# One change in two places: each transposed tile of the joint attention slots is evicted in one step, and the operands of the last pass are prepared in half-size sums on VectorE with the plain ones on ScalarE and Pool

## The chip, the cores and the metric

The kernel runs on one core of one Trainium2 chip. The metric is the time of one execution in microseconds (us), as the device reports it; the median of the runs counts. TensorE is written PE (its weight loads PEld), VectorE DVE, ScalarE ACT, GpSimd POOL, SyncE SP.

## The reference

Causal attention over 4 batches and 8 heads of 576 tokens and 64 dimensions, with a linear memory beside it, and then a mixture of four experts over the 2304 tokens that come out. Cut to what matters:

```python
scores = scale * q @ k.T            # causal, per batch and head
a = softmax(scores)
q_p = phi(q)                        # elu(q) + 1
mem_out = (q_p @ M_prev) / (q_p @ z_prev + 1e-6)
x = g * mem_out + (1 - g) * (a @ v) # g = sigmoid(beta), per head
...
p = domain_probs / domain_probs.sum(-1)
for e in range(4):                  # x is 2304 x 512, w1 512 x 1024, w2 1024 x 512
    out += p[:, e:e+1] * (relu(x @ w1[e]) @ w2[e])
```

Inputs and outputs are float32. TensorE works on fp32r operands, so an operand is split into a high part and a low part (the value less its high part), and a product is summed from high x high, high x low and low x high.

## The kernel before, in words

The program is written out by hand, one stream of calls, and each engine runs its own instructions in the order in which they are written. Two things are woven together.

**The expert work.** Tokens lie in tiles of 128. Ten tiles form five groups of two, which are worked in 24 phases (a phase is one half of one expert's 1024 columns), and the eight tiles left, 1024 tokens, are worked in a last pass of 8 phases, here called the last pass (`tail_phase`). A phase of a group is `mm1` (tiles `h`, line 851; ACT writes the high part `hh`, line 860, DVE the low part `hl`, line 861), then `mm2` (tiles `y`, line 881; DVE adds to `acc`, line 899). `h` and `y` take turns in three PSUM buffers. Weights arrive by DMA in four buffers `stg`; ACT or POOL writes their high parts `w1h`, `w2h`, and POOL their low parts `w1l`, `w2l` (line 249).

**The attention work** is a list of steps with a slot number and a priority (the table `PR`, the calls of `ev`); sorted by these, they are dealt out between the parts of the phases in proportion to their estimated costs. A *joint* task is one pair of heads over the first two tiles of a batch: 4 slots, and 12 such tasks run one after the other. Each transposes keys (`tk`), queries (`tq`) and mapped queries (`tp`) into a PSUM tile. All of these and the output tile `o` share the tag `to`, which has two buffers, so each takes the buffer of the one before the last. `split_q` and `split_k` evict such a tile: ACT writes the high parts at once, and return a function `lo` with which DVE later writes the low parts (lines 371, 374, 387). A later step runs it. The scores `sp` are reduced on DVE (line 486), ACT takes the exponential (line 500), DVE normalises (line 522), PE transposes into `pt` (line 359), ACT writes `pth` (line 542) and DVE `ptl` (line 543). `j_o` (lines 553 and 557) multiplies by the values; ACT copies half of `o` to `otmp` (line 571), and `add` on DVE (line 584) adds the halves into the tokens.

**The operands of the last pass.** The first product of the last pass is taken with 7 block products instead of 8 on the four quarter blocks of the 1024 tokens. `x_ops` prepares their operands during the last two grouped phases, where only one group is left: three plain ones (`A11`, `A12`, `A22`) and four sums or differences (`S1` to `S4`), each 128x1024 and each with a high part (`put`, a copy) and a low part (a subtraction). In the same stretch `wt_prep` sums and splits the last pass's weights (`tsum`, `wth`, `wtl`). Each product of the last pass goes into a tile `tc`, which ACT copies to `trow` (line 1060).

The call that places the pieces of `x_ops` is this:

```python
for z, (cost, part) in enumerate(ph):
    if z % 3 == 2 and pieces:
        pieces.pop(0)()
```

Of the kernel before, what the change touches and what calls it, by code (L numbers as in the profile page):

```python
# [36 lines left out]
    "o": 7,  # L37
    "jn": [1, -0.45],
    "jp": [2, 7],
    "jlo": 9,  # L40
    "jo": [4, 3],
    "wpe": 1500,
    "wvec": 400,
# [14 lines left out]
def tile_attention_moe(  # L58
# [75 lines left out]
    def f(ap):  # L134
        return ap.bitcast(F32)
# [263 lines left out]
    def t_trq(t):  # L399
        pt = to_tile(f"tq{t.i}")  # L400
        qk, last = t.qk, t.nk == NCH
        w = len(t.cs) * P
        for i in range(len(t.cs)):

            tr(pt[:, i * P : (i + 1) * P], flat(t.nat["q"][:, i]), P)
        if last:
            tr(pt[:, w : w + P], flat(t.nat["k"][:, 4]), P)
        t.lo_q = [split_q(pt, qk["qa"], qk["qb"], w, SCALE)]
        if last:
            t.lo_q.append(split_k(pt[:, w:], qk, 4 * P, D))  # L410
            t.lo_q.append(lambda: dup_k(qk, 4 * P, D))
        t.lo_q.append(lambda: dup_q(qk, w, last))

    def dup_q(qk, w, last):
        for h, (x, q_) in enumerate(((A, qk["qa"]), (Bh, qk["qb"]))):
            nc.sync.dma_start(
                out=f(qk["qz"][x, h * GW : (h + 1) * GW]), in_=f(q_[x, 0:GW])
            )
            if last:
                o = 2 * GW + h * D  # L420
                nc.sync.dma_start(out=f(qk["qz"][x, o : o + D]), in_=f(q_[x, w - D : w]))
# [319 lines left out]
    def run(fns):  # L741
        for fn in fns:
            fn()

    seen = set()
    for t in tasks:
        s0 = t.s0
        ld = s0 - 9 if t.i < 1 else s0 - 7
        PQ = PR
        if t.run not in seen:  # L750
            seen.add(t.run)
            ev(s0 - 9, 9, lambda r=t.run: batch_load(r))
# [12 lines left out]
        ev(s0 + PQ["trk"][0], 0.5, lambda t=t: run(t.lo_k))
        ev(
            s0 + PQ["trk"][0] + 1,
            -0.7,
            lambda t=t: dup_k(t.qk, 0, min(t.nk, NCH - 1) * P),
        )  # L770
# [210 lines left out]
    def x_ops():  # L981

        X, s_ = tail["x"], tail["s"]
        s3 = tail["r"][:, 0:2]


        def put(n, src, eng):
            hi, lo = X[n]
            eng.tensor_copy(hi, src)
            eng.tensor_tensor(lo, src, f(hi), ALU.subtract)  # L990

        def plain(n, i, k):
            return [lambda: put(n, a_blk(i, k), nc.vector)]

        def summed(n, eng, dst, a, b, op):
# [5 lines left out]
        return (
            plain("A11", 0, 0)
            + summed("S1", nc.vector, s_, a_blk(1, 0), a_blk(1, 1), ALU.add)
            + summed("S2", nc.vector, s_, s_, a_blk(0, 0), ALU.subtract)
            + summed("S4", nc.vector, s_, a_blk(0, 1), s_, ALU.subtract)
            + summed("S3", nc.vector, s3, a_blk(0, 0), a_blk(1, 0), ALU.subtract)
            + plain("A12", 0, 1)
            + plain("A22", 1, 1)
        )
# [367 lines left out]
    with tc.manual_schedule():  # L1377
# [43 lines left out]
        for n, ph in enumerate(phases):  # L1421
# [53 lines left out]
```

## Time and profile before

| what | value |
|---|---|
| median of 3 runs | 1061.68 us (1061.44 to 1062.12) |
| profiled execution, its own time | 1062.06 us |
| its span in the trace | 1060.3 us |
| PE busy | 998.6 us, 94% |
| DVE busy | 691.1 us, 65% |
| ACT, POOL busy | 542.2 and 545.7 us, 51% each |
| mean granted clock of TensorE | 0.977 of full speed |

Busy time is the time in which an engine has an instruction under way; a matmul's end is modelled, and matmuls overlap. The granted clock is the share of TensorE's full speed that it was given. The span is the time between the first and the last record; 1.8 us of the execution's own time lie outside it.

### The profile page before, as it was taken

The page shows a single profiled execution, that of the slowest core. Times are in us where ns is not written, and L with a number is a line of the kernel's source. Part 1 is how long each engine was busy: PE and PEld are TensorE (multiplying, and loading weights), DVE is VectorE, ACT ScalarE, POOL GpSimd, SP SyncE. Part 2 cuts the span into 40 slices and gives each one's busy share as a digit, 9 for nine tenths or more (in the row PEclk, how much of TensorE's full clock was granted, in tenths as well). Part 3 has the DMA queues.
Part 4 walks back from the last instruction along what each step waited for, and adds up shares of the span by engine and source line. Part 5 has one row for each costly group of instructions (what it writes and reads, how often), then busy time and mean ns, then how long its engine had stood idle before and what let it go on. Part 6 is the DMA issues. An engine that isn't in the chain of part 4 may idle for free.

```text
span 1060.3 us, 15727 instructions
## 1 busy us (share of the span) xinstructions
PE 998.6 (94%) x5072; PEld 830.6 (78%) x5072; DVE 691.1 (65%) x1613; ACT 542.2 (51%) x1240; POOL 545.7 (51%) x593
## 2 busy tenths in 40 slices
PE   5887888998999999999999999978999999999998
PEld 3666767877888887888888888866888888888886
DVE  5776788887776777778777766498444444543532
ACT  4666655665766666667666666434242241331320
POOL 4757665566446574555665455576335245235220
PEclk8989889999999999999999999989999999999999
DMA  5546534455453445444544432344112112112102
GB/s 135 135 125 160 145 108 128 116 137 139 116 134 107 110 115 136 115 108 106 160 117 114 107 101 68 100 130 129 50 50 70 40 41 80 40 40 73 29 19 79
DMA packets 192513, 106.33 MB, mean 100 GB/s; under 512 B 99632, under 2 KB 170800, under 8 KB 192432
## 3 DMA queue, kind: packets, MB, share of 16 engines
q1 hardware_dynamic: 191760, 105.07, 36.4%
q8 instruction: 40, 0.66, 0.3%
q14 instruction: 41, 0.34, 0.1%
q10 hardware_dynamic: 672, 0.27, 0.1%
HBM read 90.09 MB, written 4.72 MB: 89 GB/s over the span
## 4 chain that ended last, share of the span: by engine, by line
PE 74%; DVE 14%; POOL 3%; ACT 3%; issue 2%; DMA 2%; SPq 1%; ACTq 0%; POOLq 0%; DVEq 0%
PE y L881 17%; PE yt L1100 16%; PE h L851 13%; PE tc_1X L1049 4%; PE tc_0X L1049 4%; PE pt L359 3%; PE o L724 3%; PE sp L613 3%; PE tc_1Y L1049 2%; PE tc_0Y L1049 2%; DVE s L522 2%; DVE hl L861 1%; DMA stg<-in_moe_w_dram 1%; POOL w2l L249 1%; PE tc_0Z L1049 1%
## 5 line engine op out<-in xcount | busy, mean ns | idle before, releaser
L249 POOL TENSOR_TENSOR w1l<-stg,w1h 128x512 fp32r<-128x512 f32 x96 | 127.8, 1338 | 199.6 <-ACT w1h L246 194.7
L249 POOL TENSOR_TENSOR w2l<-stg,w2h 128x512 fp32r<-128x512 f32 x128 | 170.5, 1334 | 30.8 <-ACT w2h L246 22.1
L851 PE MATMUL h<-xh,w1h 128*128 128x512 f32 (+1 forms) x384 | 149.5, 389 | 0.4 <-DVE acc L899 0.4
L881 PE MATMUL y<-w2h,hh 128*128 128x512 f32 x320 | 139.2, 435 | 1.5 <-DVE hl L861 1.5
L851 PE MATMUL h<-xh,w1l 128*128 128x512 f32 (+1 forms) x384 | 138.4, 361 | 0.0
L851 PE MATMUL h<-xl,w1h 128*128 128x512 f32 (+1 forms) x384 | 138.1, 360 | 0.0
L881 PE MATMUL y<-w2h,hl 128*128 128x512 f32 x320 | 129.3, 404 | 7.2 <-DVE hl L861 7.2
L881 PE MATMUL y<-w2l,hh 128*128 128x512 f32 x320 | 128.6, 402 | 2.9 <-POOL w2l L249 2.9
L1113 DVE SCALAR_TENSOR_TENSOR xt<-yt,pn,xt 128x512 f32<-128x512 f32 x56 | 42.0, 751 | 87.0 <-PE yt L1100 87.0
L861 DVE SCALAR_TENSOR_TENSOR hl<-h,hh 128x512 fp32r<-128x512 f32 (+1 forms) x96 | 57.6, 600 | 62.8 <-ACT hh L860 61.9
L248 POOL TENSOR_SCALAR w2h<-stg 128x512 fp32r<-128x512 f32 x104 | 65.2, 627 | 58.2 <-PE yt L1100 45.2
L656 ACT ACTIVATE s<-s,st 128x384 f32<-128x384 f32 (+2 forms) x80 | 55.1, 688 | 72.0 <-DVE st L651 71.7
L851 PEld LDWEIGHTS h<-xh,w1l 128*128 128x128 f32 x384 | 73.6, 192 | 11.0
L851 PEld LDWEIGHTS h<-xh,w1h 128*128 128x128 f32 x384 | 74.5, 194 | 7.2 <-ACT qb L368 0.6
L881 PEld LDWEIGHTS y<-w2h,hl 128*128 128x128 f32 x320 | 61.6, 192 | 22.3 <-DVE hl L861 8.6
L851 PEld LDWEIGHTS h<-xl,w1h 128*128 128x128 f32 x384 | 74.4, 194 | 5.4
L860 ACT ACTIVATE hh<-h 128x512 fp32r<-128x512 f32 (+1 forms) x96 | 50.3, 524 | 53.4 <-PE h L851 52.5
L899 DVE SCALAR_TENSOR_TENSOR acc<-y,pn,acc 128x512 f32<-128x512 f32 x70 | 52.3, 747 | 37.6 <-PE y L881 37.2
L881 PEld LDWEIGHTS y<-w2l,hh 128*128 128x128 f32 x320 | 62.3, 195 | 11.9 <-POOL w2l L249 4.7
L359 PE MATMUL pt<-ident,s 128*128 128x128 f32 (+1 forms) x376 | 62.5, 277 | 8.0 <-DVE s L522 4.6
L881 PEld LDWEIGHTS y<-w2h,hh 128*128 128x128 f32 x320 | 62.0, 194 | 10.1 <-DVE hl L861 2.1
L359 PEld LDWEIGHTS pt<-ident,s 128*128 128x128 f32 (+1 forms) x376 | 46.4, 141 | 27.4 <-issue 9.0
(297 smaller groups left out, 2591.5 us busy)
## 6 DMA issues: line engine op xcount, KB each, us to landing
stg<-in_moe_w_dram SPq DMA_DIRECT2D x256, 256.0 KB, 2.9
natall<-in_k_dram SPq DMA_DIRECT2D x34, 128.0 KB, 2.6
natall<-in_v_dram SPq DMA_DIRECT2D x32, 128.0 KB, 3.0
natall<-in_q_dram SPq DMA_DIRECT2D x60, 64.0 KB, 2.6
out_dram<-acc SPq DMA_DIRECT2D x10, 256.0 KB, 2.1
kha<-kha SPq DMA_DIRECT2D x16, 128.0 KB, 2.4
khb<-khb SPq DMA_DIRECT2D x16, 128.0 KB, 2.3
natall<-in_k_dram SPq DMA_DIRECT2D x28, 64.0 KB, 2.5
```

The costliest lines, as they stand in the source:

```text
L248: nc.gpsimd.tensor_scalar(hi, t, 1.0, 1.0, ALU.mult, ALU.mult)
L249: nc.gpsimd.tensor_tensor(lo, t, f(hi), ALU.subtract)
L359: nc.tensor.transpose(dst, src, ident[0:n, 0:n])
L656: nc.scalar.activation(s.s[:, 0:w], s.s[:, 0:w], AF.Copy, scale=s.st[:, 3:4])
L851: nc.tensor.matmul(pt[0][:, cols], lhsT=w_[:, c], rhs=x_[:, c, cols], start=(c == 0 and z == 0), stop=(c == NKD - 1 and z == 2),)
L860: nc.scalar.activation(h_, pt[0][:, cols], AF.Relu)
L861: nc.vector.scalar_tensor_tensor(l_, pt[0][:, cols], 0.0, f(h_), ALU.max, ALU.subtract)
L881: nc.tensor.matmul(pt[0], lhsT=h_[fc][:, tk], rhs=w_, start=(fc == 0 and z == 0), stop=(fc == HF - 1 and z == 2),)
L899: nc.vector.scalar_tensor_tensor(acc[g, tt], pt[0], pe, acc[g, tt], ALU.mult, ALU.add)
L1049: nc.tensor.matmul(bank[b][:, 0:TB], lhsT=w_[:, n, cs], rhs=x_[:, c], start=first and c == 0 and z == 0, stop=c == 1 and z == 2, skip_grou ...
L1100: nc.tensor.matmul(o, lhsT=h_[fc][:, tk], rhs=w_, start=(z == 0 and fc == p and y == 0), stop=(z == 1 and fc == p + 2 and y == 2),)
L1113: nc.vector.scalar_tensor_tensor(acc_, o, pe, acc_, ALU.mult, ALU.add)
```

## The change

In the joint slots the eviction of a tile is no longer divided between two places of the list: the step with the low parts gets the priority of the transposes (`lo_q`, `lo_k`, `lo_qp`, and `lo` of `pt`), and `add` follows `j_o` in its slot instead of the next one. The mapped queries are transposed a slot later (`jtrqp`). The DMAs of `dup_q` become a step of their own. The other attention tasks keep their places. In `x_ops` each sum is made in two halves of 128x512 on DVE, three instructions each; the high parts of the plain operands are copied by ACT, their low parts subtracted by POOL; the pieces are now 30 instead of 11, and two are placed in every three parts of a phase.

```diff
+    "jtrqp": [2, 2.5],
...
-    "jlo": 9,
...
         if last:
             t.lo_q.append(split_k(pt[:, w:], qk, 4 * P, D))
-            t.lo_q.append(lambda: dup_k(qk, 4 * P, D))
-        t.lo_q.append(lambda: dup_q(qk, w, last))
 
     def dup_q(qk, w, last):
+        if last:
+            dup_k(qk, 4 * P, D)
...
-        ev(s0 + PQ["trq"][0], PQ["trq"][1], lambda t=t: t_trq(t), 109.0 * len(t.cs))
-        ev(s0 + PQ["trq"][0] + 1, 0.4, lambda t=t: run(t.lo_q))
-        ev(s0 + PQ["trk"][0], PQ["trk"][1], lambda t=t: t_trk(t), 109.0 * t.nk)
-        ev(s0 + PQ["trk"][0], 0.5, lambda t=t: run(t.lo_k))
...
+        (q0, q1), (k0, k1), j_ = PQ["trq"], PQ["trk"], t.joint
+        ev(s0 + q0, q1, lambda t=t: t_trq(t), 109.0 * len(t.cs))
+        ev(*((s0 + q0, q1) if j_ else (s0 + q0 + 1, 0.4)), lambda t=t: run(t.lo_q))
+        ev(s0 + q0 + 1, 0.45, lambda t=t: dup_q(t.qk, len(t.cs) * P, t.nk == NCH))
+        ev(s0 + k0, k1, lambda t=t: t_trk(t), 109.0 * t.nk)
+        ev(s0 + k0, k1 if j_ else 0.5, lambda t=t: run(t.lo_k))
...
-        ev(s0 + PQ["trqp"][0], PQ["trqp"][1], lambda t=t: t_trqp(t), 109.0 * len(t.cs))
-        ev(s0 + PQ["trqp"][0], 4.5, lambda t=t: run(t.lo_qp))
+        p0, p1 = PQ["jtrqp" if j_ else "trqp"]
+        ev(s0 + p0, p1, lambda t=t: t_trqp(t), 109.0 * len(t.cs))
+        ev(s0 + p0, p1 if j_ else 4.5, lambda t=t: run(t.lo_qp))
...
-            ev(i + PQ["jp"][0], PQ["jlo"], lambda i=i: run(slots[i].lo))
+            ev(i + PQ["jp"][0], PQ["jp"][1], lambda i=i: run(slots[i].lo))
...
-                ev(i + PQ["jo"][0] + 1, -0.6, lambda i=i: run(slots[i].add))
+                ev(i + PQ["jo"][0], PQ["jo"][1], lambda i=i: run(slots[i].add))
...
+        vec = nc.vector.tensor_tensor
+        plain = {"A11": a_blk(0, 0), "A12": a_blk(0, 1), "A22": a_blk(1, 1)}
+
+        def hi(n):
+            return [lambda: nc.scalar.activation(X[n][0], plain[n], AF.Copy)]
+
+        def lo(n):
             return [
+                lambda: nc.gpsimd.tensor_tensor(X[n][1], plain[n], f(X[n][0]), ALU.subtract)
             ]
...
+        def summed(n, dst, a, b, op):
+            h_, l_ = X[n]
+            return [
+                fn
+                for k in range(2)
+                for fn in (
+                    lambda k=k: vec(dst[:, k], a[:, k], b[:, k], op),
+                    lambda k=k: nc.vector.tensor_copy(h_[:, k], dst[:, k]),
+                    lambda k=k: vec(l_[:, k], dst[:, k], f(h_[:, k]), ALU.subtract),
+                )
+            ]
...
+        other = hi("A11") + hi("A12") + lo("A11") + hi("A22") + lo("A12") + lo("A22")
+        out_ = []
+        for z, fn in enumerate(sums):
+            out_.append(fn)
+            if z % 4 == 3:
+                out_ += [other.pop(0)]
+        return out_ + other
...
-                if z % 3 == 2 and pieces:
+                if z % 3 and pieces:
                     pieces.pop(0)()
```

**The order on DVE in a joint task.** A stretch of DVE's row in the joint part of the program before the change, from the low parts of one tile to the next normalisation (`tq` holds queries, `tp` mapped queries, `xr` the tokens):

```order
L371 SCALAR_TENSOR_TENSOR qpa_86<-tp_1042,qpa_86 64x256
L374 SCALAR_TENSOR_TENSOR qpb_87<-tp_1042,qpb_87 64x256
L486 ISA s_1078,st_1079<-sp_1080,mask 128x256
L486 ISA st_1079 128x1
L486 ISA s_1078,st_1079<-sp_1080,mask 128x256
L486 ISA st_1079 128x1
L861 SCALAR_TENSOR_TENSOR hl_113<-h_2_1066,hh_109 128x256
L371 SCALAR_TENSOR_TENSOR qa_91<-tq_1061,qa_91 64x256
L374 SCALAR_TENSOR_TENSOR qb_92<-tq_1061,qb_92 64x256
L861 SCALAR_TENSOR_TENSOR hl_114<-h_3_1096,hh_110 128x256
L543 TENSOR_TENSOR ptl_100<-pt_1139,pth_99 128x2x128
L584 TENSOR_TENSOR xr<-o_1104,otmp_1115 64x256 x2
```

And the same twelve places on DVE in the changed program:

```order
L371 SCALAR_TENSOR_TENSOR qa_91<-tq_1042,qa_91 64x256
L374 SCALAR_TENSOR_TENSOR qb_92<-tq_1042,qb_92 64x256
L486 ISA s_1067,st_1068<-sp_1069,mask 128x256
L486 ISA st_1068 128x1
L486 ISA s_1067,st_1068<-sp_1069,mask 128x256
L486 ISA st_1068 128x1
L861 SCALAR_TENSOR_TENSOR hl_113<-h_2_1061,hh_109 128x256
L371 SCALAR_TENSOR_TENSOR qpa_86<-tp_1093,qpa_86 64x256
L374 SCALAR_TENSOR_TENSOR qpb_87<-tp_1093,qpb_87 64x256
L861 SCALAR_TENSOR_TENSOR hl_114<-h_3_1098,hh_110 128x256
L584 TENSOR_TENSOR xr<-o_1107,otmp_1118 64x256 x2
L543 TENSOR_TENSOR ptl_100<-pt_1141,pth_99 128x2x128
```

The low parts of `tq` and `tp` have changed places, and `add` (line 584) stands ahead of `ptl` (line 543) instead of behind it.

**The order on POOL at the end of the grouped phases.** Before the change, from the first weights of the last grouped phase on:

```order
L249 TENSOR_TENSOR w1l_116<-stg_8037,w1h_115 128x512
L249 TENSOR_TENSOR w1l_118<-stg_8059,w1h_117 128x512
L249 TENSOR_TENSOR w1l_120<-stg_8080,w1h_119 128x512
L249 TENSOR_TENSOR w1l_122<-stg_8099,w1h_121 128x512
L249 TENSOR_TENSOR w2l_124<-stg_8103,w2h_123 128x512
L249 TENSOR_TENSOR w2l_126<-stg_8124,w2h_125 128x512
L249 TENSOR_TENSOR w2l_128<-stg_8128,w2h_127 128x512
L249 TENSOR_TENSOR w2l_130<-stg_8149,w2h_129 128x512
```

In the changed program the same stretch of POOL's row reads:

```order
L249 TENSOR_TENSOR w1l_116<-stg_8039,w1h_115 128x512
L249 TENSOR_TENSOR w1l_118<-stg_8061,w1h_117 128x512
L993 TENSOR_TENSOR A11l<-xt,A11h 128x1024
L249 TENSOR_TENSOR w1l_120<-stg_8082,w1h_119 128x512
L249 TENSOR_TENSOR w1l_122<-stg_8103,w1h_121 128x512
L249 TENSOR_TENSOR w2l_124<-stg_8107,w2h_123 128x512
L249 TENSOR_TENSOR w2l_126<-stg_8128,w2h_125 128x512
L249 TENSOR_TENSOR w2l_128<-stg_8132,w2h_127 128x512
L993 TENSOR_TENSOR A12l<-xt,A12h 128x1024
L249 TENSOR_TENSOR w2l_130<-stg_8153,w2h_129 128x512
L993 TENSOR_TENSOR A22l<-xt,A22h 128x1024
```

Three subtractions of 128x1024 now stand among the weights' low parts, two of them ahead of weights that TensorE still needs in that phase.

**The order on DVE in the same stretch.** Before the change, from the first piece of `x_ops` on:

```order
L989 CAST A11h<-xt 128x1024
L990 TENSOR_TENSOR A11l<-xt,A11h 128x1024
L861 SCALAR_TENSOR_TENSOR hl_111<-h_0_8000,hh_107 128x256
L997 TENSOR_TENSOR xsum<-xt 128x1024
L861 SCALAR_TENSOR_TENSOR hl_112<-h_1_8021,hh_108 128x256
L989 CAST S1h<-xsum 128x1024
L990 TENSOR_TENSOR S1l<-xsum,S1h 128x1024
L997 TENSOR_TENSOR xsum<-xsum,xt 128x1024
L861 SCALAR_TENSOR_TENSOR hl_113<-h_2_8043,hh_109 128x256
```

In the changed program the same stretch of DVE's row reads:

```order
L1003 TENSOR_TENSOR xsum<-xt 128x512
L1004 CAST S1h<-xsum 128x512
L861 SCALAR_TENSOR_TENSOR hl_111<-h_0_8000,hh_107 128x256
L1005 TENSOR_TENSOR S1l<-xsum,S1h 128x512
L1003 TENSOR_TENSOR xsum<-xt 128x512
L861 SCALAR_TENSOR_TENSOR hl_112<-h_1_8022,hh_108 128x256
L1004 CAST S1h<-xsum 128x512
L1005 TENSOR_TENSOR S1l<-xsum,S1h 128x512
L1003 TENSOR_TENSOR xsum<-xsum,xt 128x512
L861 SCALAR_TENSOR_TENSOR hl_113<-h_2_8044,hh_109 128x256
```

Ahead of the third `hl` stood six instructions of 128x1024; now seven of 128x512 stand there.

## Rows read from the trace of the kernel before

**Rows 1.** The page, busy time (us, share of the span, instructions) of each engine.

```profile
PE 998.6 (94%) x5072; PEld 830.6 (78%) x5072; DVE 691.1 (65%) x1613; ACT 542.2 (51%) x1240; POOL 545.7 (51%) x593
```

**Rows 2.** Windows of 100 us: length, busy by engine, granted clock, DMA.

```profile
100.00:200.00 100.00, 86.91 (x483) 73.42 (x481) 81.03 (x212) 60.20 (x163) 65.29 (x77) 0.93 0.47 128
...
700.00:800.00 100.00, 90.34 (x400) 73.96 (x401) 64.92 (x83) 32.64 (x56) 48.87 (x44) 0.95 0.27 81
```

**Rows 3.** Groups of PE, 50 to 252 us: busy, mean ns, idle before, releaser.

```profile
L359 PE MATMUL pt<-ident,s 128*128 128x128 f32 x72 | 13.2, 292 | 4.6 <-DVE s L522 4.6
...
L553 PE MATMUL o<-qpa,ms 128*128 128x256 f32 x12 | 4.8, 398 | 17.8 <-DVE qpb L374 17.8
```

**Rows 4.** Groups of DVE by form, 50 to 252 us.

```profile
L584 DVE TENSOR_TENSOR xr<-o,otmp 64x256 f32<-64x256 f32 x22 | 9.2, 416 | 0.2
...
L543 DVE TENSOR_TENSOR ptl<-pt,pth 128x256 fp32r<-128x256 f32 x12 | 5.0, 421 | 7.6 <-ACT pth L542 7.6
...
L374 DVE SCALAR_TENSOR_TENSOR qb<-tq,qb 64x256 fp32r<-64x256 f32 x11 | 4.7, 426 | 0.2
```

**Rows 5.** Timelines (start, length) around one joint output, and another wait.

```profile
106.32 0.43 DVE L374 SCALAR_TENSOR_TENSOR qpb<-tp,qpb 64x256 fp32r<-64x256 f32 x1
106.90 0.36 PE L553 MATMUL o<-qpa,ms 128*128 128x256 f32 x1 [2.02 <-DVE qpb L374]
108.28 0.77 ACT L571 ACTIVATE otmp<-o 64x256 f32<-64x256 f32 x2 [2.82 <-PE o L557]
...
111.60 0.42 DVE L543 TENSOR_TENSOR ptl<-pt,pth 128x256 fp32r<-128x256 f32 x1 [1.35 <-ACT pth L542]
111.94 0.84 DVE L584 TENSOR_TENSOR xr<-o,otmp 64x256 f32<-64x256 f32 x2
...
123.52 0.55 PE L553 MATMUL o<-qpa,ms 128*128 128x256 f32 x1 [2.85 <-DVE qpb L374]
```

**Rows 6.** Short windows: length, busy by engine, granted clock, DMA.

```profile
100.00:110.00 10.00, 7.59 (x62) 7.24 (x61) 7.16 (x21) 6.29 (x15) 8.93 (x11) 1.00 0.61 173
...
120.00:130.00 10.00, 7.15 (x37) 6.97 (x36) 6.57 (x15) 4.95 (x15) 3.64 (x4) 0.66 0.50 142
...
700.00:715.00 15.00, 9.58 (x32) 7.20 (x33) 14.83 (x14) 1.95 (x4) 10.54 (x5) 0.66 0.40 118
```

**Rows 7.** Timelines of POOL and DVE, 698 to 727 us.

```profile
698.28 1.72 POOL L249 TENSOR_TENSOR w2l<-stg,w2h 128x512 fp32r<-128x512 f32 x1
698.90 2.18 DVE L990 TENSOR_TENSOR S1l<-xsum,S1h 128x1024 fp32r<-128x1024 f32 x1
699.97 2.24 POOL L249 TENSOR_TENSOR w2l<-stg,w2h 128x512 fp32r<-128x512 f32 x1
701.12 2.17 DVE L997 TENSOR_TENSOR xsum<-xsum,xt 128x1024 f32<-128x1024 f32 x1
...
714.18 0.68 DVE L989 CAST S3h<-trow 128x1024 fp32r<-128x1024 f32 x1
714.90 1.23 DVE L990 TENSOR_TENSOR S3l<-trow,S3h 128x1024 fp32r<-128x1024 f32 x1
...
715.92 1.36 POOL L249 TENSOR_TENSOR w2l<-stg,w2h 128x512 fp32r<-128x512 f32 x1 [5.38 <-ACT w2h L246]
...
726.02 0.69 DVE L1031 TENSOR_TENSOR wtl<-stg,wth 128x512 fp32r<-128x512 f32 x1
```

**Rows 8.** Timelines of PE and ACT from 703 us to the last pass.

```profile
703.68 0.79 PE L881 MATMUL y<-w2h,hl 128*128 128x512 f32 x1 [3.12 <-DVE hl L861]
...
707.57 0.79 PE L881 MATMUL y<-w2h,hl 128*128 128x512 f32 x1 [2.25 <-DVE hl L861]
...
724.37 0.50 PE L881 MATMUL y<-w2h,hl 128*128 128x512 f32 x1 [1.81 <-DVE hl L861]
...
730.62 1.06 ACT L1030 ACTIVATE wth<-tsum 128x1024 fp32r<-128x1024 f32 x1 [2.59 <-DVE tsum L1027]
...
732.21 0.50 PE L1049 MATMUL tc_0X<-S2h,wth 128*128 128x512 f32 x1 [1.19 <-ACT trow L1060]
```

More of the change, by code (lines that the diff above doesn't have):

```diff
@@ L761, in tile_attention_moe @@
         ev(s0 + PQ["phi3"][0] + 1, 2, lambda t=t: t_phi4(t))
-        ev(s0 + PQ["trq"][0], PQ["trq"][1], lambda t=t: t_trq(t), 109.0 * len(t.cs))
-        ev(s0 + PQ["trq"][0] + 1, 0.4, lambda t=t: run(t.lo_q))
-        ev(s0 + PQ["trk"][0], PQ["trk"][1], lambda t=t: t_trk(t), 109.0 * t.nk)
-        ev(s0 + PQ["trk"][0], 0.5, lambda t=t: run(t.lo_k))
[L766 to L770, printed above, removed]
+        (q0, q1), (k0, k1), j_ = PQ["trq"], PQ["trk"], t.joint
[4 more added lines that the diff above has]
+        ev(s0 + k0, k1 if j_ else 0.5, lambda t=t: run(t.lo_k))
+        ev(s0 + k0 + 1, -0.7, lambda t=t: dup_k(t.qk, 0, min(t.nk, NCH - 1) * P))
         ev(s0, PQ["v"], lambda t=t: t_v(t))
-        ev(s0 + PQ["trqp"][0], PQ["trqp"][1], lambda t=t: t_trqp(t), 109.0 * len(t.cs))
-        ev(s0 + PQ["trqp"][0], 4.5, lambda t=t: run(t.lo_qp))
+        p0, p1 = PQ["jtrqp" if j_ else "trqp"]
+        ev(s0 + p0, p1, lambda t=t: t_trqp(t), 109.0 * len(t.cs))
+        ev(s0 + p0, p1 if j_ else 4.5, lambda t=t: run(t.lo_qp))
     for i, s in slots.items():
@@ L984, in x_ops @@
         s3 = tail["r"][:, 0:2]
[L987 to L995, printed above, removed]
+        vec = nc.vector.tensor_tensor
[3 more added lines that the diff above has]
+        def lo(n):
             return [
-                lambda: eng.tensor_tensor(dst, a, b, op),
-                lambda: put(n, dst, eng),
-            ]
[L1001 to L1008, printed above, removed]
-        )
+                lambda: nc.gpsimd.tensor_tensor(X[n][1], plain[n], f(X[n][0]), ALU.subtract)
+            ]
+        def summed(n, dst, a, b, op):
[9 more added lines that the diff above has]
+            ]
+        sums = (
+            summed("S1", s_, a_blk(1, 0), a_blk(1, 1), ALU.add)
+            + summed("S2", s_, s_, a_blk(0, 0), ALU.subtract)
+            + summed("S4", s_, a_blk(0, 1), s_, ALU.subtract)
+            + summed("S3", s3, a_blk(0, 0), a_blk(1, 0), ALU.subtract)
+        )
+        other = hi("A11") + hi("A12") + lo("A11") + hi("A22") + lo("A12") + lo("A22")
[5 more added lines that the diff above has]
+        return out_ + other
     def wt_prep(i):
```

## Prediction

> **What bounds the kernel now.** I read the busy times first: PE is under way for 998.6 us of the 1060.3 us span, every other engine for two thirds or less [rows 1]. So the time is PE's work, plus what PE waits, plus what a lowered clock adds, and an edit on DVE, ACT or POOL is worth what it does to PE's waits. The windows of 100 us say where these are: from 100 to 200 us PE is busy 86.9 us at a granted clock of 0.93, from 700 to 800 us 90.3 us at 0.95 [rows 2]. The first window lies in the joint tasks, the second holds the passage from the grouped phases to the last pass. The change touches both and little else.
>
> In the joint tasks the reader should see one large group: PE waits 17.8 us ahead of the first matmul of `o`, over 12 outputs, and the releaser is the low part `qpb` of a mapped-query tile on DVE; ahead of `pt` it waits 4.6 us for the normalisation [rows 3]. `o` does not read that `qpb`, which belongs to a later task. It wants the PSUM buffer: `tp`, `tq` and `o` take two `to` buffers in turn, so `o` gets the one that `tp` held. The timeline shows it: `qpb` ends at 106.75 and `o` starts at 106.90, having waited 2.02 us [rows 5].
>
> Some waits cost twice. In the window with the 2.85 us wait at 123.52 [rows 5] the granted clock is 0.66, so for 68% of it the clock stood at 1.2 instead of 2.4 GHz: 10 us x 0.34 = 3.4 us of PE's work lost. In the window with the 2.02 us wait the clock stayed at 1.00 [rows 6].
>
> In the passage, PE waits for `hl` on DVE three times, 3.12, 2.25 and 1.81 us, and 1.19 us for `trow` on ACT at the start of the last pass [rows 8]; the clock there is 0.66 over 15 us, at most 5.1 us lost [rows 6]. The `hl` are late because `x_ops` stands ahead of them on DVE.
>
> **The change part by part, joint tasks.** *The wait of `o` is not removed.* With the new order (`tk`, `tq`, `tp`, `o`) `o` takes the buffer that `tq` held. On DVE the low parts of `tq` now stand at the very places where those of `tp` stood, behind the same normalisation, and they cost the same, 0.43 us each [rows 4, 5]. PE reaches `o` after the same transposes and scores as before. So I cost the exchange at 0; the other end is the whole 17.8 us, a rival below.
>
> *What does move is `add`.* It cost 0.84 us behind `ptl`, and `ptl` waits on DVE for `pth`, 7.6 us over 12 [rows 4]. In the shown task `otmp` ends at 109.05 but `add` starts only at 111.94, after `ptl` has waited 1.35 us until 111.60 [rows 5]. In the new order `add` runs within that wait, and DVE is free 0.84 us sooner. The next wait of `o` ends when DVE has worked off the queue between, so it ends that much sooner too. Bounds: 0, and the 7.6 us of waits that can be filled. I take 0.84/1.35 of it, the share filled in the shown task: 7.6 x 0.62 = **-4.7 us**. What is late next is DVE itself, which is busy 81 of 100 us [rows 2].
>
> *The clock.* 2.85 us shortened by 0.84 is 2.01 us, the length of the wait that kept its clock. I take one such drop avoided, **-3.4 us**; bounds 0 and four of them (-13.6), since I have a price for one.
>
> *`lo_k` ahead of the score reduction.* The two low parts of the keys (2 x 0.43 us) now precede line 486, so the exponential, then `pth` on ACT, can come 0.85 us later. DVE's `rn` sums and the previous `ptl` lie between that reduction and the normalisation, and cover it. Without that cover it would be 12 x 0.85 = 10.2 us. I take one task in twelve exposed, **+0.9 us**. The separate step of `dup_q` adds an entry to the list and no instruction, and its DMAs keep their place behind the high parts: 0. `tp` is now evicted just ahead of `add`; its high parts stand on ACT ahead of `otmp`, so nothing queues behind them that did not before.
>
> **The passage.** Here DVE and POOL hold each other up. A `w2l` on POOL ends at 700.00, and `S1l` on DVE, started at 698.90, ends 1.08 us after it; the next `w2l` ends 1.13 us after that, at 702.21, and `xsum` 1.08 us later [rows 7]. They take turns. Alone the same instructions take 1.23 us on DVE and 1.36 us on POOL, a 128x1024 copy 0.68 us [rows 7]. So the stretch is as long as the turns of both together. A copy's turn I set at 0.68 less the 0.15 us that the subtraction's turn is shorter: 0.53 us.
> - Before: 11 sums or subtractions x 1.08, 7 copies x 0.53, 12 weight low parts x 1.13 = 11.9 + 3.7 + 13.6 = 29.2 us.
> - After: 8 x 1.08 and 4 x 0.53 on DVE (in halves), on POOL 13.6 and three subtractions of twice 1.13: 8.6 + 2.1 + 13.6 + 6.8 = 31.1 us.
>
> DVE sheds three subtractions and three copies, but POOL's are dearer than those it replaces: **+1.9 us**. The bounds: if DVE and POOL did not hold each other up, DVE would shed 3 x (1.23 + 0.68) = 5.7 us, and the `hl` waits (7.2 us) would shrink by that: -5.7; if POOL's three subtractions (no row shows one) all lay on the path, +6.8. The three copies on ACT are about 1.06 us each, by the copy of that size there [rows 8]; they stand ahead of `hh` that nobody waits for yet.
>
> The Trainium skill, Perfetto Trace Analysis, section Optimizing Scalar/DVE Operations, says that work moved between VectorE and GpSimd may not help, because they share a read port of SBUF. By that rule the term is the +1.9 of the turns, without it the -5.7; the trace agrees with the rule, 2.18 us against 1.23.
>
> *Halves.* A 128x512 subtraction takes 0.69 us, two 1.38 against 1.23 [rows 7]: 12 more instructions at 0.15 us are 1.8 us, nothing where the excess falls into POOL's turn. I take half, **+0.9 us**. The gain of halves is that an `hl` waits behind less. I leave it out: DVE's last `hl` ends when the turns do, and `trow` waits for the weights' `wth`, whose sums on DVE now also have pieces of `S3` ahead of them. The first wait (3.12 us) should shrink, and new ones come later, for PSUM buffers behind `acc` and for the `w2l` behind `A12l`.
>
> **Sum.** -4.7 - 3.4 + 0.9 + 1.9 + 0.9 = -4.4 us on the profiled execution's 1062.06 us, which is 0.38 us above the median of the runs: 1057.7, so a median of **1057.3 us**.
>
> **The rivals.**
> - *Nothing shows.* The `add` finishes sooner but DVE then waits for `pth` or `hh` as long as before, and the passage is even: 1061.7 us. For it: DVE also waits for other releasers in these tasks, so time given to it may be idle again. Against it: between `add` and the next `o` of the shown kind DVE has a full queue.
> - *The wait of `o` goes away*, because the low parts now directly follow their transpose and DVE runs further ahead: 1061.7 - 17.8 = 1043.9 us, less with the clock. Against it: the same DVE places as before.
> - *DVE and POOL do not meet as counted*, since the pieces are spread over nearly all parts of the phases: joint tasks as forecast (-7.2), passage -5.7: 1048.8 us.
> - *Slower: the three subtractions on POOL.* `A12l` stands ahead of the last `w2l` and `A22l` runs against the last `S3` pieces. PE waits for that `w2l`, the wait of about 3 us drops the clock, and the last pass starts late. Price: 6.8 us, and up to 5.1 us of clock again. With joint tasks unchanged, 1068.5 us. It decides once what it adds exceeds the 7.2 us of the joint tasks; below that the total is still a gain.
>
> **How the numbers follow.** Chances: forecast 0.43 (its own range, 1051 to 1059.5: from all 7.6 us filled and two clock drops avoided, -7.6 - 6.8 + 3.7 = -10.7 us, to the smallest gain that can be told), nothing shows 0.20, the wait of `o` gone 0.09, no turns 0.10, slower 0.18. A range from 1046 to 1066 us holds the forecast, no change, no turns and the milder half of the slow case, about 0.82. About 0.2% (2.1 us) can be told from no change in this kernel: faster 0.62, same 0.20, slower 0.18.
>
> **What would show it.** Right: the group of `o` still waits, now for `qb` on DVE, by 10 to 16 us; `ptl` (128x256) waits less than 7.6 us; the granted clock from 100 to 200 us is above 0.93. In the passage, POOL's three subtractions take 2.3 to 4.5 us each, the `hl` waits move from the first phase to the second, and the last pass starts within 3 us of where it did. Wrong: if `o` waits under 5 us, the exchange did more than I cost; if `add` waits long on DVE for `otmp` and `hl` behind it is late, it did harm; if the last pass starts 5 us earlier or later than the joint part explains, the turns are miscounted.

## The result, and the profile after

The changed kernel takes 1050.68 us (median of 4 runs, 1050.62 to 1052.01), the kernel before 1061.56 us on the same chip (4 runs, 1059.24 to 1062.12). The ratio is 0.9905, with a 95% interval from 0.9887 to 0.9922: faster by 10.9 us, where 4.4 us were forecast. The direction holds, and so does the range of 1046 to 1066 us; the size was forecast too small by more than half, and the time lies 0.3 us below the forecast's own range of 1051 to 1059.5 us. The kernel before scatters by itself: over all chips used its single runs took 1054.2 to 1065.6 us, those under 1056 us at a mean granted clock of 0.984 to 0.990 and those over 1062 us at 0.975 to 0.981, so that one profiled run shows a change of less than 5 us only if it lies near its median.

The page of the changed kernel, busy time of each engine, beside [rows 1]:

```profile
PE 994.1 (95%) x5072; PEld 828.9 (79%) x5072; DVE 687.4 (66%) x1619; ACT 544.7 (52%) x1243; POOL 549.1 (52%) x596
```

PE is under way 4.5 us less for the same 5072 matmuls; the rest of the gain is shorter waits. The windows tell where. First the kernel before, from the first matmul of its first phase to that of its ninth, where the joint tasks end, and a window of 10 us that was not shown (length, busy by engine, granted clock, DMA):

```profile
40.71:253.49 212.78, 184.92 (x1035) 156.28 (x1034) 168.99 (x447) 127.99 (x343) 131.54 (x159) 0.94 0.49 132
...
140.00:150.00 10.00, 6.55 (x22) 5.29 (x22) 6.29 (x13) 3.47 (x10) 4.34 (x4) 0.67 0.26 79
```

The changed kernel, the same stretch and the windows that answer to [rows 2, 6]:

```profile
40.36:239.45 199.09, 179.50 (x1035) 153.43 (x1034) 159.19 (x445) 126.74 (x342) 131.60 (x160) 0.96 0.53 139
...
100.00:200.00 100.00, 91.41 (x505) 77.86 (x506) 81.92 (x232) 61.59 (x169) 65.24 (x77) 0.95 0.49 132
100.00:110.00 10.00, 8.46 (x48) 7.91 (x49) 6.80 (x19) 5.52 (x16) 6.30 (x9) 0.83 0.55 144
120.00:130.00 10.00, 9.34 (x61) 8.37 (x61) 6.72 (x16) 7.01 (x19) 6.07 (x7) 0.91 0.59 162
140.00:150.00 10.00, 10.00 (x49) 8.25 (x48) 7.46 (x22) 5.66 (x18) 6.15 (x9) 0.88 0.49 122
```

The joint part has become 13.7 us shorter. PE's idle time in it falls from 212.78 - 184.92 = 27.9 us to 19.6 us, and its 1035 matmuls are under way 5.4 us less: the clock, which was at half speed for most of two windows (0.66 and 0.67), stays at 0.88 or above in both. It falls elsewhere, to 0.83 from 100 to 110 us, where the kernel before had 1.00 [rows 6]; over the whole joint part it is 0.96 instead of 0.94. How much of this is the change and how much the scatter of the clock was not separated. The distance between the two kernels is 14.0 us at the start of phase 22 (691.62 against 677.59 us). From there to the first matmul of the last pass's product with `S2` it took 40.6 us before and takes 43.4 us now. So the traced span, 11.4 us shorter, is 13.7 us less in the joint part, 0.3 us less ahead of it and 2.8 us more in the passage.

PE's groups in the changed kernel, 50 to 240 us, beside [rows 3]:

```profile
L359 PE MATMUL pt<-ident,s 128*128 128x128 f32 x72 | 12.4, 281 | 0.0
...
L553 PE MATMUL o<-qpa,ms 128*128 128x256 f32 x12 | 4.2, 354 | 16.5 <-DVE qb L374 13.4 <-DVE kl L387 3.0
```

`o` waits nearly as long as before, now for `qb` and once for `kl`; the wait of `pt` for the normalisation is gone. DVE's groups, first the normalisation in the kernel before, 50 to 252 us:

```profile
L522 DVE TENSOR_SCALAR s<-s,st 128x128 f32<-128x128 f32 x24 | 15.5, 686 | 0.4
...
L522 DVE TENSOR_SCALAR s<-s,st 128x256 f32<-128x256 f32 x24 | 13.5, 604 | 0.4
```

Then the changed kernel, 50 to 240 us, beside [rows 4]:

```profile
L522 DVE TENSOR_SCALAR s<-s,st 128x128 f32<-128x128 f32 x24 | 10.9, 494 | 0.4
...
L522 DVE TENSOR_SCALAR s<-s,st 128x256 f32<-128x256 f32 x24 | 10.3, 473 | 0.4
L584 DVE TENSOR_TENSOR xr<-o,otmp 64x256 f32<-64x256 f32 x22 | 9.2, 420 | 2.1 <-ACT otmp L571 1.8
...
L543 DVE TENSOR_TENSOR ptl<-pt,pth 128x256 fp32r<-128x256 f32 x12 | 5.0, 421 | 4.0 <-ACT pth L542 3.9
```

`add` now stands in a place where DVE waited, and the wait of `ptl` has fallen from 7.6 to 4.0 us. The same 48 normalisations take 7.8 us less; the last section comes back to that.

### The profile page after: what moved, and what is told of

It reads as the page before. It is cut to its first block, busy times and chain, and to the rows that moved or that the text cites. A ratio compares the mean times of both kernels' runs of the same rounds, so it can differ in the third digit from the quotient of the medians.

```text
span 1048.9 us, 15746 instructions
## 1 busy us (share of the span) xinstructions
PE 994.1 (95%) x5072; PEld 828.9 (79%) x5072; DVE 687.4 (66%) x1619; ACT 544.7 (52%) x1243; POOL 549.1 (52%) x596
## 4 chain that ended last, share of the span: by engine, by line
PE 79%; DVE 10%; POOL 3%; ACT 3%; DMA 2%; issue 2%; SPq 1%; ACTq 0%; POOLq 0%; DVEq 0%
PE y L881 17%; PE yt L1112 17%; PE h L851 16%; PE tc_1X L1061 4%; PE tc_0X L1061 4%; PE pt L359 4%; PE o L724 3%; PE sp L613 3%; PE tc_1Y L1061 2%; PE tc_0Y L1061 2%; POOL w2l L249 1%; PE tc_1Z L1061 1%; PE tc_0Z L1061 1%; DVE hl L861 1%; PE o L557 1%
## 5 line engine op out<-in xcount | busy, mean ns | idle before, releaser
L249 POOL TENSOR_TENSOR w1l<-stg,w1h 128x512 fp32r<-128x512 f32 x96 | 125.7, 1316 | 190.6 <-ACT w1h L246 174.9
L249 POOL TENSOR_TENSOR w2l<-stg,w2h 128x512 fp32r<-128x512 f32 x128 | 167.6, 1311 | 27.6 <-ACT w2h L246 18.9
L662 DVE TENSOR_TENSOR ptl<-pt,pth 128x384 fp32r<-128x384 f32 (+1 forms) x96 | 51.7, 553 | 19.8 <-ACT pth L660 18.9
```

Of the source, the lines that this page charges most:

```text
L249: nc.gpsimd.tensor_tensor(lo, t, f(hi), ALU.subtract)
L662: lambda x=x: nc.vector.tensor_tensor(x[2], x[0], f(x[1]), ALU.subtract) for x in groups
```

## The experiments

Times are medians; the ratios are to the kernel before on the same chip. Its median was 1060.16 us on the chip of e1 to e4, 1061.87 on that of e5, e6, e7 and e9, 1061.01 on that of e8 and e10 to e12, and 1060.32 on that of e13 and e14, so a difference between runs of two chips carries these differences too. The two columns on the right are from each kernel's one trace: the joint part, and the passage from phase 22 to the product with `S2`. The passage repeats well: in the nine traces with the old `x_ops` it is 40.5 to 40.8 us. The five traces with the whole joint change have joint parts of 198.7 to 200.0 us.

| run | what | us | ratio (95%) | joint | passage |
|---|---|---|---|---|---|
| | kernel before | 1061.56 | 1 | 212.8 | 40.6 |
| | changed kernel | 1050.68 | 0.9905 (0.9887 to 0.9922) | 199.1 | 43.4 |
| e1 | joint part alone | 1048.24 | 0.9891 (0.9869 to 0.9913) | 199.5 | 40.5 |
| e2 | `x_ops` alone | 1063.17 | 1.0030 (1.0013 to 1.0047) | 213.9 | 43.9 |
| e3 | e1, `add` late | 1058.84 | 0.9991 (0.9968 to 1.0013) | 203.7 | 40.7 |
| e4 | before, `add` early | 1053.35 | 0.9949 (0.9922 to 0.9977) | 201.5 | 40.5 |
| e5 | e1, no exchange | 1044.06 | 0.9843 (0.9808 to 0.9879) | 195.8 | 40.8 |
| e6 | e1, `lo_k` late | 1053.84 | 0.9927 (0.9905 to 0.9948) | 204.7 | 40.7 |
| e7 | e1, halves alone | 1052.08 | one run | 199.5 | 44.4 |
| e8 | e1, plain on ACT and POOL | 1049.22 | one run | 198.7 | 42.1 |
| e9 | e1, plain on ACT and DVE | 1046.36 | 0.9862 (0.9826 to 0.9898) | 200.0 | 38.3 |
| e10 | before, `lo_k` early | 1055.40 | 0.9941 (0.9918 to 0.9964) | 206.5 | 40.5 |
| e11 | e5 and e9 | 1041.85 | 0.9815 (0.9781 to 0.9849) | 195.5 | 38.2 |
| e12 | e11, normalisation on ACT | 1065.61 | 1.0054 (1.0032 to 1.0076) | 218.0 | 38.2 |
| e13 | before, `lo_k` and `add` early | 1050.76 | 0.9919 (0.9896 to 0.9942) | 202.8 | 40.5 |
| e14 | before, the other low parts early | 1057.54 | 0.9983 (0.9961 to 1.0004) | 208.4 | 40.6 |

**The two places apart.** e1 keeps `x_ops` as it was, e2 keeps the joint slots as they were.

> The joint slots as in the changed kernel, x_ops and its placing as before the change. By the traces of before and after, the joint part gave 14.0 us and the passage to the last pass took 2.8 us back. If the two parts add up, the time is 1061.6 - 14.0 = 1047.6 us, below both kernels. Rival: x_ops saves time in the passage that is hidden by another wait, then this run is at 1050.7 or above.

> x_ops in halves on three engines and its denser placing, the joint slots as before. Theory (DVE and POOL take turns, total of turns 1.9 us longer, halves 0.9 us): 1064.4 us, the last pass starts 2 to 4 us later than before. Rival (no turns, DVE sheds 5.7 us): 1056 us.

The joint changes alone gain about 12 us, the `x_ops` change alone loses about 3, so neither needs the other. The product of the two ratios, 0.9921, lies just inside the interval of the changed kernel.

**`add`.** e4 takes this one step alone, which is the edit below; e3 is e1 without it:

```diff
-                ev(i + PQ["jo"][0] + 1, -0.6, lambda i=i: run(slots[i].add))
+                ev(i + PQ["jo"][0], PQ["jo"][1], lambda i=i: run(slots[i].add))
```

> As e1_joint_alone, but the add behind o goes back to the next slot, behind ptl. Theory A (the gain comes from add, which no longer stands between ptl and the normalisation): most of the 14 us is lost, 1057 to 1062 us, and the waits of pt for the normalisation (5.5 us before, none after) come back. Theory B (the gain comes from the places of the low parts, which shift when DVE meets POOL): at most 3 us lost, 1047.6 to 1051 us.

> The kernel before with one edit: add follows j_o in its slot. Theory A (add): 1048 to 1054 us, pt waits under 1.5 us. Theory B (places of the low parts): 1058 to 1061.6 us.

Alone it is worth 0.51%, 5.4 us (6.8 us by the medians); taken out of the whole it costs 1.0%, 10.6 us by the medians. The profiled runs of e3 and e4 are the fastest of theirs (5.5 and 2.7 us under the medians), so their joint parts in the table are short by about as much; that of e2 is the slowest of its ten, 2.9 us above.

The waits of `pt`, by which both expectations meant to tell the theories apart, came out against theory A, though both times came out as it had them: 3.7 us are left in e4, where under 1.5 were expected, and 0.8 us in e3, where they should have come back. In e4 the wait of `ptl` is 3.3 us instead of 7.6, as forecast, but the first five `o` wait 14.4 us instead of 13.2. The gain lies in the other seven, which wait 0.2 us instead of 4.6. The fourth `o`, whose wait was to shrink, and its window in e4:

```profile
121.30 0.55 PE L553 MATMUL o<-qpa,ms 128*128 128x256 f32 x1 [3.52 <-DVE qpb L374]
...
120.00:130.00 10.00, 8.70 (x49) 8.73 (x50) 7.46 (x21) 5.00 (x15) 3.01 (x4) 0.66 0.53 136
```

**The exchange of `tq` and `tp`.**

```diff
-    "jtrqp": [2, 2.5],
+    "jtrqp": [1, 2.5],
```

> As e1_joint_alone, but the mapped queries are transposed in slot 1 again, ahead of the queries, so that o takes the buffer of the queries' tile as before the exchange was undone only in part. The prediction costs this exchange at nothing: 1047 to 1050 us, the same as e1_joint_alone (1048.2). Rival: the exchange is what took the waits of pt for the normalisation away and let DVE meet POOL less often (normalisations 20.9 us in e1_joint_alone, 28 to 29 us without all parts): 1054 to 1060 us and pt waits of 4 to 5 us.

Without the exchange the kernel is 4.2 us faster than e1 by the medians; by the ratios it is 0.48%, 5.1 us, and by the joint parts 3.6 us. `o` takes the buffer of the mapped queries again, as in the kernel before, and not that of the queries, as the expectation has it. The traces show one place for the loss. The timeline of the changed kernel, at the eleventh `o` (start, length), and its window there:

```profile
219.45 1.59 DVE L815 TENSOR_TENSOR xl<-xr,xh 128x512 fp32r<-128x512 f32 x2
221.05 0.55 DVE L371 SCALAR_TENSOR_TENSOR qa<-tq,qa 64x384 fp32r<-64x384 f32 x1
...
222.42 0.23 DVE L387 TENSOR_TENSOR kl<-tq,khb 64x64 fp32r<-64x64 f32 x1
...
222.80 0.36 PE L553 MATMUL o<-qpa,ms 128*128 128x256 f32 x1 [3.01 <-DVE kl L387]
```

```profile
220.00:230.00 10.00, 7.20 (x31) 6.05 (x32) 6.74 (x16) 4.18 (x12) 3.53 (x3) 0.83 0.21 60
```

And e5 at the same place:

```profile
219.85 0.28 PE L553 MATMUL o<-qpa,ms 128*128 128x256 f32 x1
```

```profile
220.00:230.00 10.00, 8.87 (x52) 7.40 (x51) 9.13 (x24) 6.49 (x18) 4.62 (x5) 1.00 0.43 116
```

The `tq` that holds the buffer there (384 queries, and 64 keys in the same tile) is that of the next, not joint, task, whose low parts still stand divided, a slot later, behind two `xl`. With the exchange `o` has to wait for that tile: 3.0 us, and the clock falls to 0.83. All seven traces with the exchange have this wait, 3.0 to 3.7 us, and no other has it. Up to that place the exchange does no harm: the tenth `o` starts at 204.87 us in e1 and at 206.21 us in e5; the twelfth at 238.71 and 235.10.

**The low parts of the keys.** e10 moves `lo_k` alone, which is the edit below; e6 is e1 with `lo_k` in its late place:

```diff
-        ev(s0 + PQ["trk"][0], 0.5, lambda t=t: run(t.lo_k))
+        ev(s0 + PQ["trk"][0], PQ["trk"][1] if t.joint else 0.5, lambda t=t: run(t.lo_k))
```

> As e1_joint_alone, but the low parts of the keys stand behind the score reduction again. The prediction costs the earlier place at +0.9 us, so this run should be the same or up to 1 us faster than e1_joint_alone: 1047 to 1048.5 us. Rival: the earlier place fills a stretch in which DVE is free and is what took the waits of pt away: then 1053 to 1059 us, with pt waits of 4 to 5 us.

> The kernel before with one edit: in the joint tasks the low parts of the keys stand ahead of the score reduction. The prediction costs this at +0.9 us; putting it back cost e6_joint_lok_late 5.6 us. If the place by itself is worth that, 1055 to 1057 us. If it only pays together with add in its new place, 1060 to 1063 us.

By the medians it is worth 5.6 us either way (by the ratios 0.59% alone and 0.36% in e6); the prediction had it as a loss of 0.9. The timeline of the kernel before in its first joint task:

```profile
48.06 0.29 DVE L486 CUSTOM_DVE_ANT_0 s<-sp,mask 128x128 f32<-128x128 f32 x1 [0.21 <-PE sp L481]
...
48.88 0.42 DVE L861 SCALAR_TENSOR_TENSOR hl<-h,hh 128x256 fp32r<-128x256 f32 x1 [0.31 <-ACT hh L860]
49.22 0.41 DVE L387 TENSOR_TENSOR kl<-tk,kha 64x256 fp32r<-64x256 f32 x1
49.64 0.43 DVE L387 TENSOR_TENSOR kl<-tk,khb 64x256 fp32r<-64x256 f32 x1
...
51.21 1.81 DVE L522 TENSOR_SCALAR s<-s,st 128x128 f32<-128x128 f32 x2
51.64 2.54 POOL L249 TENSOR_TENSOR w1l<-stg,w1h 128x512 fp32r<-128x512 f32 x2
...
69.45 0.55 PE L553 MATMUL o<-qpa,ms 128*128 128x256 f32 x1 [3.37 <-DVE qpb L374]
```

The same task in e10:

```profile
47.27 0.41 DVE L387 TENSOR_TENSOR kl<-tk,kha 64x256 fp32r<-64x256 f32 x1
47.69 0.43 DVE L387 TENSOR_TENSOR kl<-tk,khb 64x256 fp32r<-64x256 f32 x1
48.15 0.29 DVE L486 CUSTOM_DVE_ANT_0 s<-sp,mask 128x128 f32<-128x128 f32 x1
...
50.01 0.76 DVE L522 TENSOR_SCALAR s<-s,st 128x128 f32<-128x128 f32 x2
51.08 2.55 POOL L249 TENSOR_TENSOR w1l<-stg,w1h 128x512 fp32r<-128x512 f32 x2 [0.59 <-ACT w1h L246]
...
66.23 0.35 PE L553 MATMUL o<-qpa,ms 128*128 128x256 f32 x1 [2.62 <-DVE qpb L374]
```

The first matmul of the first phase stands at 40.71 us before and at 40.20 us in e10; counted from there, the reduction starts 0.60 us later, the normalisation 0.69 us earlier and `o` 2.7 us earlier. Ahead of the reduction `kl`, 0.84 us, takes the place of two waits of DVE, 0.21 us for the scores and 0.31 us for `hh`. The normalisation also takes 1.05 us less in this task: before, a `w1l` on POOL ran beside it from 51.64 us, in e10 the `w1l` starts after it, at 51.08 us.

Over all twelve tasks the gain is not in `o`, which waits 18.2 us in e10 against 17.8, and hardly in `pt`, which waits 4.0 us against 4.6. PE's waits ahead of `y`, nearly all for POOL's `w2l`, fall from 2.5 us to none, those ahead of `tq` from 1.7 us to none, and the matmuls are under way 1.7 us less. That the place of `lo_k` makes the difference is shown; how it frees `y` and `tq` is not. The rival of e6 had the right time (1053 to 1059 us), but not the waits of `pt` that it expected, 4 to 5 us: 1.0 us was measured.

**Do they add up?** e13 takes `lo_k` and `add` together, e14 the three other low parts (`lo_q`, `lo_qp`, `lo` of `pt`) without either. Both edit the calls of `ev` in the diff of the change and leave `tp` in its old slot; in e14 the DMAs of `dup_q` are a step of their own too.

> Kernel before, with two single edits together: the low parts of the keys ahead of the score reduction (alone 0.9941, about -5.6 us) and the output's add in its own slot (alone 0.9949, about -5.4 us). If the two act on different waits they add up: -11 us, about 1050 us, ratio 0.9896. If each gives DVE the same idle place, the second adds little: -6 to -7 us, about 1054 us. If they need each other (together they are the whole gain of the joint part without the exchange of the transposes): -16 to -17 us, about 1044 us.

> Kernel before with the other three divided evictions joined in the joint tasks (low parts of queries, mapped queries and of the transposed scores right behind their transposes), without the early low parts of the keys, the early add, or the exchange of the transposes. If the gains of single edits add up to the -17 us that all of them give without the exchange, these low parts are worth the rest: -17 + 5.6 + 5.4 = -6 us, about 1055 us, ratio 0.9943. If the two named edits need each other and these are bystanders: within 2 us of the kernel before, about 1061 us.

e13 gains 0.81%, less than the 1.10% of the sum of its two edits, which lies just outside its interval; by the medians it is 9.6 us. e14 gains 0.17%, 2.8 us by the medians, and its interval reaches just past 1. The product of the three ratios, 0.9941 x 0.9949 x 0.9983 = 0.9873, lies inside the interval of e5. So the single gains explain e5 within what was measured; whether the 3 us between 0.9873 and 0.9843 are an interplay stays open. The wait of `pt` looks like one: 4.6 us before, it is 3.7, 4.0 and 3.3 us with one of the edits (e4, e10, e14), 2.6 us in e13, 1.4 us in e5 and none in the changed kernel.

**The passage, edit by edit** (all with the joint part as in e1). e9 and e8 make the high parts of the plain operands on ACT, the low parts on DVE (e9) or POOL (e8); e7 makes the sums in halves and places two pieces in three parts of a phase, the plain operands being whole on DVE. Of the lines below the first is that of e9 and e8, the second of e9, the third of e8, and the last two of e7, whose `summed` is that of the change:

```diff
+                    nc.scalar.activation(hi, src, AF.Copy),
+                    nc.vector.tensor_tensor(lo, src, f(hi), ALU.subtract),
...
+                    nc.gpsimd.tensor_tensor(lo, src, f(hi), ALU.subtract),
...
-                if z % 3 == 2 and pieces:
+                if z % 3 and pieces:
```

> As e1_joint_alone, but the high parts of the three plain operands on ACT; their low parts stay on DVE, whole, and the sums are whole. This takes three copies off DVE and puts nothing on POOL: turns 29.2 - 3 x 0.53 = 27.6 us. Expected: the passage 39.0 us instead of 40.5, the time 1046.6 us. Rival: the passage is set by the weights' sums and their DMA, then no change (40.5 us, 1048.2).

> As e1_joint_alone, but only the plain operands move (high parts to ACT, low parts to POOL); the sums stay whole and the pieces 11 in every third part. By the turns of DVE and POOL (three subtractions of 2.26 us more on POOL, 3 x 1.08 and 3 x 0.53 less on DVE) the passage is 40.5 + 1.9 = 42.4 us. If only the spreading in halves does harm, as in e7_halves_alone (44.4), it is 40.5 us or less.

> As e1_joint_alone, but the sums of x_ops in halves with two pieces in every three parts; the plain operands stay whole on DVE. Measure: from the first h of the phase of the first piece to the first matmul of S2, 40.6 us before, 43.4 in the changed kernel. Turns of DVE and POOL unchanged, 12 more instructions: 41 to 42 us. Rival (smaller pieces let hl through and save PE's waits): 38 us or less. Other rival (spreading the pieces to the end of the phases is what delays the weights' sums): 43 us.

Copies on ACT gain 2.2 us of the passage. The same with the low parts on POOL loses 1.6 us, so these three subtractions cost 3.8 us more on POOL than on DVE. The halves with their denser placing lose 3.9 us, more than the expectation of that run gave to either cause; the two were not tried apart. DVE's groups in e7 in the passage:

```profile
L1003 DVE TENSOR_TENSOR S1l<-xsum,S1h 128x512 fp32r<-128x512 f32 x2 | 3.3, 1654 | 0.1
...
L1002 DVE CAST S1h<-xsum 128x512 fp32r<-128x512 f32 x2 | 2.3, 1168 | 0.0
```

And in the timeline of e9, where the sums are whole:

```profile
683.93 1.45 DVE L989 CAST S1h<-xsum 128x1024 fp32r<-128x1024 f32 x1
685.41 2.19 DVE L990 TENSOR_TENSOR S1l<-xsum,S1h 128x1024 fp32r<-128x1024 f32 x1
```

The same copy takes 2.3 us in halves and 1.45 us whole, the same subtraction 3.3 and 2.2 us (1.44 and 2.18 us in e1): each half of `S1` met a subtraction on POOL anew. The halves of `S4`, most of which met none, took 0.43 us for a copy and 0.69 us for a subtraction. The Trainium skill, Perfetto Trace Analysis, section Optimizing Scalar/DVE Operations, says that breaking up instructions may let work finish sooner where an unsaturated engine makes others wait. Here PE did wait for DVE's `hl`, but DVE was saturated (busy 14.83 of 15.00 us in the kernel before [rows 6], 42.44 of the 44.36 us in e7), so the condition is not met and no run here tests it: the passage took 40.5 us whole and 44.4 us in halves.

**The best of both.** e11 joins e5 and e9; e12 then moves the normalisation from DVE to ACT.

> e5_joint_tp_early (mapped queries transposed in slot 1) and e9_plain_act_dve (high parts of the plain operands on ACT, nothing more on POOL) together. If the joint part and the passage add up, 1044.1 - 1.9 = 1042.2 us, with a passage of 38 to 39 us.

e11 is faster than both kernels: by 1.85% than the one before, and by 8.8 us than the changed one by their medians.

```diff
-            nc.vector.tensor_scalar(s.s3[:, hd], s.s3[:, hd], r[:, hd : hd + 1], None, ALU.mult)
+            nc.scalar.activation(s.s3[:, hd], s.s3[:, hd], AF.Copy, scale=r[:, hd : hd + 1])
```

> As e11_both_best, but the normalisation of the joint tasks runs on ACT instead of DVE, so that none of these 48 instructions can meet POOL on DVE. Theory (DVE's time behind POOL is what PE waits for): o waits fall from 13 to under 7 us and the time to 1032 to 1039 us. Rival (DVE being busy is not what sets the waits; ACT, which also holds otmp and the high parts, becomes late instead): 1042 us or more, with PE waits released by ACT.

A group of ACT in e12, 50 to 230 us:

```profile
L522 ACT ACTIVATE s<-s,st 128x128 f32<-128x128 f32 (+1 forms) x43 | 17.2, 447 | 33.7 <-DVE st L516 33.7
```

ACT stands waiting for DVE's reciprocal ahead of the normalisation, and all that is queued on ACT waits with it; `o` then waits 26.8 us in the joint part instead of 13.8. Less work on DVE (its busy time in the joint part falls from 159.5 to 137.8 us) is no gain when it puts a wait at the head of ACT's queue.

## Why the prediction was wrong in its size, point by point

The step that failed is the part on `lo_k`: forecast as a loss of 0.9 us, it is a gain of about 5.6 us (e10, e6). Beside it the three other low parts were put into no term, and the exchange was costed at 0 and loses about 4 us.

- **What bounds the kernel: right.** PE's waits in the joint tasks and in the passage, and the clock behind them, hold the whole difference.
- **"The wait of `o` is not removed": right.** 16.5 us are left of 17.8, 13.4 us of them for `qb` (10 to 16 us were forecast), and the rival with the wait gone falls.
- **"So I cost the exchange at 0": wrong.** It costs 4.2 us. The step looked at the joint task shown, where it holds, and not at the last joint tasks, whose next task is not joint and keeps its late low parts.
- **`add`, -4.7 us: right on DVE and about right in size, not in its place on PE.** `ptl` waits 4.3 us less in e4, as forecast, and the time falls by 5.4 us, what the clock gives back included; within the whole it is more. But the wait that was to shrink, of the fourth `o`, grew from 2.85 to 3.52 us, and the gain came in the last seven tasks. That the size fits is in part luck.
- **The clock, -3.4 us: right in direction, by a step that does not hold.** The trace shows 5.4 us less for the same matmuls; one drop was priced, and the trace held a second, from 140 to 150 us. The step took the length of the wait as what decides: 2.85 us lost the clock, 2.02 us kept it. In the changed kernel the third `o` waits 2.09 us at 101.55 us in a window at 0.83, and the fifth 3.58 us in a window at 0.95, with 0.88 in the next. In e4 the wait was not shortened, and both windows stay at 0.66.
- **"`lo_k` ahead of the score reduction", +0.9 us: the step with the wrong sign.** It is -5.6 us. I asked whether the reduction would be late, and not what DVE did before it: in the task shown it waited 0.52 us. Nor did I ask who stands behind the old place: the normalisation, which comes 0.69 us earlier. By which waits of PE this becomes 5.6 us stays open: those of `y` and `tq` went, that of `o` did not. The 4.6 us of `pt` [rows 3] were named and put into no term; they went only with the edits together.
- **The three other low parts, not priced:** -2.8 us alone by the medians, not told apart from nothing.
- **The passage, +2.8 us: right to 0.1 us**, by counting turns, but luckier than it looks. Taken after POOL's share the halves cost 1.3 us, alone they cost 3.9 us (e7), where 0.9 was forecast; that the terms add up to 2.8 us rests on an interplay that no term has.

The third and the fifth `o` of the changed kernel, and the window of the fifth:

```profile
101.55 0.55 PE L553 MATMUL o<-qpa,ms 128*128 128x256 f32 x1 [2.09 <-DVE qb L374]
137.33 0.35 PE L553 MATMUL o<-qpa,ms 128*128 128x256 f32 x1 [3.58 <-DVE qb L374]
...
130.00:140.00 10.00, 6.42 (x36) 5.20 (x35) 9.26 (x25) 6.21 (x17) 7.17 (x8) 0.95 0.45 130
```

PE in the passage of the changed kernel, beside [rows 8]:

```profile
684.18 0.50 PE L881 MATMUL y<-w2h,hh 128*128 128x512 f32 x1 [0.68 <-DVE hl L861]
688.97 0.80 PE L881 MATMUL y<-w2h,hl 128*128 128x512 f32 x1 [2.68 <-DVE hl L861]
...
710.88 0.79 PE L881 MATMUL y<-w2h,hl 128*128 128x512 f32 x1 [4.84 <-DVE hl L861]
...
720.99 0.50 PE L1061 MATMUL tc_0X<-S2h,wth 128*128 128x512 f32 x1 [1.15 <-ACT trow L1072]
```

POOL there, beside [rows 7]:

```profile
689.67 2.55 POOL L993 TENSOR_TENSOR A11l<-xt,A11h 128x1024 fp32r<-128x1024 f32 x1
...
703.23 2.56 POOL L993 TENSOR_TENSOR A12l<-xt,A12h 128x1024 fp32r<-128x1024 f32 x1
705.76 1.71 POOL L249 TENSOR_TENSOR w2l<-stg,w2h 128x512 fp32r<-128x512 f32 x1
707.43 2.78 POOL L993 TENSOR_TENSOR A22l<-xt,A22h 128x1024 fp32r<-128x1024 f32 x1
```

As forecast the subtractions take 2.3 to 4.5 us each (2.55 to 2.78), the long `hl` wait has moved into the second phase (4.84 us), and PE waits for the `hl` that stands behind DVE's turns with `A12l` and `A22l`, not for the `w2l`. Of the terms, POOL's share is 1.6 us (e8; forecast 1.9) and the halves on top of it 1.3 us (43.4 less 42.1; forecast 0.9).

So the joint part was forecast at -7.2 us and is -11.6 us by the ratio of e1. By the ratios of the single runs this is -6.3 for `lo_k`, -5.4 for `add` and +5.1 for the exchange, which leaves -5 for the three other low parts and interplay, of which e14 shows -1.8.

## What to carry to other kernels

An instruction moved ahead of one that waits costs only what exceeds the wait, and what stood behind its old place gains up to its time (0.69 of 0.84 us in the task shown): price a reordering at both places. Where buffers are taken in turn, check a new order at the first and last turns, where the neighbour is of another kind. Where two engines hold each other up, count instructions and not bytes: here a split, placed more densely, made more meetings, and a copy moved to a third engine removed one.

## What the runs showed of the hardware that was not expected

Short DVE instructions pay for meeting POOL by the instruction. In the changed kernel the timeline of DVE and POOL in the passage has:

```profile
688.84 1.16 DVE L1004 CAST S2h<-xsum 128x512 fp32r<-128x512 f32 x1
...
698.33 0.41 DVE L1004 CAST S4h<-xsum 128x512 fp32r<-128x512 f32 x1
698.37 1.53 POOL L249 TENSOR_TENSOR w2l<-stg,w2h 128x512 fp32r<-128x512 f32 x1 [2.77 <-ACT w2h L246]
...
708.05 2.45 DVE L1004 CAST S3h<-trow 128x512 fp32r<-128x512 f32 x1
```

The same copy takes 0.41 us where it starts 0.04 us ahead of a `w2l` on POOL, 1.16 us where a `w1l` is under way, and 2.45 us where `A22l` is, which runs from 707.43 to 710.21 us. The `hl` in the same stretch, which read PSUM and one tile of SBUF, keep their 0.41 us. The Trainium skill, SBUF — State Buffer, section Who interferes with whom, says that a copy in the mode with both port pairs and GpSimd block each other for a whole instruction, and that a VectorE instruction with at most one SBUF input, outside those modes, does not contend; these rows agree. The normalisations of the joint tasks behave so too: their mean fell from 686 and 604 ns to 494 and 473 ns without any change to them, 7.8 us of DVE's time. Of the 48, 36 overlapped a POOL instruction before (mean 754 ns) and 29 do now (584 ns); in either kernel no normalisation without such an overlap took more than 355 ns. How much of the gain is this and how much the order alone was not separated.
